# Attention of a fused kernel in a fixed order on every engine, with fixed PSUM banks and keys scaled in place

## The chip, the cores and the metric

The kernel runs on one core of a Trainium2 chip. The metric is the time of one execution on the device in microseconds (us); lower is better. The engines are PE (TensorE), DVE (VectorE), ACT (ScalarE), POOL (GpSimd) and SP (SyncE, which issues most DMAs). L12 means line 12 of the kernel, of before or of the change as the sentence says.

## The reference

A causal linear attention with a decay for each head comes first. Its output, laid out as 4 × 768 rows of 512, goes through a Fourier mix, a normalisation and an MLP.

```python
# attention: q, k, v are (4, 8, 768, 64), lam (8,); blocks of 64 rows
for b in range(nb):
    intra = einsum(qb, kb) * Dmask[None]                # Dmask = lam ** (i - j) for i >= j
    intra = einsum(intra, vb)
    inter = einsum(qb * lam_pow[None], kv_state)
    out[:, :, sl] = intra + inter
    kv_state = lam_block * kv_state + einsum(kb * rev_pow[None], vb)
# mix: x is (4, 768, 512), w_ch1 (512, 2048), w_ch2 (2048, 512)
mixed = np.real(fft(fft(x, axis=1), axis=2))
u = x + mixed
un = (u - mean(u)) / sqrt(var(u) + 1e-6)
return u + np.maximum(un @ w_ch1, 0.0) @ w_ch2
```

The two weights arrive as float64 and are converted to float32 on the chip.

## The kernel before

**Attention** runs in twelve steps: step i is batch i // 3, rows 256 (i % 3) to 256 (i % 3) + 255, as two chunks of 128 rows. For one step PE does:

- `turn_k`, `turn_q` (L349, L356): 16 transposes of keys and queries; ACT copies them out (L350, L357), and DVE makes the decayed queries (L361, L363);
- `to_state` (L369): products of the scaled keys `kd` with v, which DVE adds to the state (L380; L377 for the first chunk of a batch). POOL scales the old state by the decay of a chunk ahead of that (L379). There are three state buffers in turn;
- `from_state` (L399): decayed queries with the state of before, which opens the output's PSUM tile `po`;
- `scores` (L384): keys with queries in four PSUM tiles, which DVE masks with the decay (L390) into `sc`;
- `within` (L405): masked scores with v, added into `po`; ACT copies the result out (L411 and the lines behind it);
- `back` (L425): transposes of the output of the step before; ACT writes the halves into x (L435, L436).

POOL prepares a step in `apart`: it copies keys and queries into layouts split by even and odd rows (L341, 1024 elements wide; ACT does it for step 0) and writes the scaled keys into the one buffer `kd` (L343). SP loads k, q and v, 512 KB each (L330), up to three steps ahead, into three rotating buffers `ld` and two for v.

**What is woven in.** Between these pieces the program emits other work: the Fourier mix of batch 0 (`fft_ln`: folds on DVE L549 to L637; matmuls along the sequence L670; along the width L682 to L687; sums L758 to L771; statistics and normalisation L701 to L722; transposes L727); the conversion of the weights, 32 *words* of 512 KB (five DVE instructions L230, L234, L236, L238, L239 and two of ACT, L229 and L232, for each); and the first half of the MLP (`mlp`: L816 first product, L830 second, L860 and L861 the sums). `mixed` and `beside` interleave the generators by weights, of which each `yield` states how much work it stands for.

**What sets the order.** The program order is that of emission, and a scheduler may move instructions unless `tc.keep_in_program_order` pins them. Before, only the first product of each group on PE and some instructions of DVE are pinned. `tc.high_priority` favours the instructions behind which PE waits.

**PSUM.** There are eight banks, in two pools: `pa` with five and `pm` with three tiles in rotation. Attention, Fourier mix and MLP take them in turn; `psum_t` chooses the pool by a count.

**Behind attention** the rest of the first half of the MLP runs beside the Fourier mix of batches 1 to 3 and the remaining words, and then the second half and the other products. PE stays in one stream to the end (L1265, L1191 and L1098 are matmuls there).

Of the kernel before, what the change touches and what calls it, by code (L numbers as in the profile page):

```python
# [19 lines left out]
EPS = 1e-6  # L20
# [57 lines left out]
def kernel(  # L78
# [44 lines left out]
    ld = front_pool("ld", 3)  # L123
# [14 lines left out]
    cnt = [0]  # L138

# [3 lines left out]

    def psum_a(shape):
        return new(pa, shape, "pa")

    def psum_m(shape):
        return new(pm, shape, "pm")
# [5 lines left out]
    nc.scalar.dma_start(lamb, lam.rearrange("(o h) -> o h", o=1).broadcast_to([128, H]))  # L154
# [5 lines left out]
    nc.gpsimd.memset(pulse, 0.0)  # L160
    for hd in HD:
        nc.vector.tensor_copy(pulse[hd, 1:C + 1:2], ident[hd, hd])
    decay = const.tile([128, H, C + 1], F32, name="decay")
    for h in range(H):
        scan(decay[:, h, :], lamb[:, h:h + 1].broadcast_to([128, C + 1]), pulse, 0.0, op0=ALU.mult, op1=ALU.add)

    lamq = const.tile([128, HP], F32, name="lamq")
    for hi in range(2):
        nc.vector.tensor_copy(lamq[HD[hi]], lamb[HD[hi], hi::2])
    qpow = const.tile([128, HP, C], F32, name="qpow")  # L170
    for hp in range(HP):
        scan(qpow[:, hp, :], lamq[:, hp:hp + 1].broadcast_to([128, C]), ident, 1.0, op0=ALU.mult, op1=ALU.bypass)
# [3 lines left out]
    nc.gpsimd.memset(cvt, -896.0 * 16 * 8)  # L176
    mhalf = const.tile([128, G], F32, name="mhalf")
    nc.gpsimd.memset(mhalf, -0.5)
# [19 lines left out]
    def load_tables(i):  # L198
        if i == 1:
            nc.sync.dma_start(cs, cn["cs"].ap())  # L200
            nc.sync.dma_start(ix, cn["ix"].ap())
        elif i == 2:
            nc.sync.dma_start(dt, cn["dt"].ap())

    def load_weights(dst, src):

        if src.dtype == F32:
            nc.sync.dma_start(dst, src)
            yield 1.0
            return  # L210
        if landed[0] < NW // 2:
            raw = hp_.tile([128, 2 * WP], U32, tag="hr", name=f"raw{cnt[0]}")
        else:
            raw = ld.tile([128, 2 * WP], U32, tag="kqv", name=f"raw{cnt[0]}")
        e = ep.tile([128, 2 * WP], U16, tag="e", name=f"e{cnt[0]}")
        pw, sg = e[:, 0:WP], e[:, WP:2 * WP].bitcast(BF16)
        cnt[0] += 1
        nc.sync.dma_start(raw, src.bitcast(U32))
        if LAG[0] <= landed[0] < LAG[1] or NW // 2 <= landed[0] < NW // 2 + 2:
            yield 0.5  # L220
# [3 lines left out]


        held_back = LAG[0] <= landed[0] < LAG[1] or NW // 2 <= landed[0] < NW // 2 + 2
        landed[0] += 1
        pin = tc.keep_in_program_order if late_words else lambda i: i
# [1292 lines left out]
```

## Time and profile before

| what | value |
|---|---|
| runs | 818.54, 813.4, 814.37 us; median 814.37 us |
| profiled execution | 816.04 us, its span 814.3 us, mean PE clock 0.972 of full speed |
| busy, share of the span | PE 756.0 us (93%), DVE 612.6 us (75%), ACT 225.6 us (28%), POOL 195.9 us (24%) |
| instructions | 17075 |
| DMA | 123.50 MB, mean 152 GB/s |

The profile shows one execution. A busy time is a union of intervals, and a matmul of the program leaves two records on PE. Line numbers in it are those of the kernel before. An idle time is put down to what ended last before the waiting instruction started. The granted clock of PE is given for any stretch of time as a share of full speed.

### The profile page before, as it was taken

What the parts mean: (1) busy time and instruction counts of PE and PEld (TensorE: products, weight loads), DVE (VectorE), ACT (ScalarE), POOL (GpSimd) and SP (SyncE); (2) the same over time, 40 slices, a digit from 0 to 9 for tenths busy, and PEclk for the clock granted to TensorE, in tenths of its full rate; (3) what the DMA queues carried; (4) which work ended last, traced back from release to release, by engine and by line L of the source; (5) the groups of instructions that cost most, each with busy time, mean ns of one, the idle gap of its engine ahead of it and who ended that gap; (6) DMA issues with size and microseconds to landing.
All of it is one profiled execution on the core that took longest, in us unless ns stands there. A gap on an engine that the chain in (4) does not pass through costs nothing.

```text
span 814.3 us, 17075 instructions
## 1 busy us (share of the span) xinstructions
PE 756.0 (93%) x6872; PEld 657.1 (81%) x6872; DVE 612.6 (75%) x1173; ACT 225.6 (28%) x512; POOL 195.9 (24%) x215
## 2 busy tenths in 40 slices
PE   4796777969999998999999999999999999999997
PEld 3785767757658676865974789999999999999997
DVE  4568678973199767846695699978997599758984
ACT  3462434552236211100200122103420343123410
POOL 4433241420000120421100693244012200330013
PEclk9798998988999998999999999999999999999999
DMA  9764645461345244742143236667554556455442
GB/s 260 237 177 126 181 138 183 144 221 59 126 140 178 75 97 110 226 98 97 57 88 89 79 142 214 221 222 230 176 182 129 178 174 182 134 175 172 131 144 77
DMA packets 119220, 123.50 MB, mean 152 GB/s; under 512 B 40174, under 2 KB 79726, under 8 KB 119142
## 3 DMA queue, kind: packets, MB, share of 16 engines
q1 hardware_dynamic: 111792, 103.13, 43.3%
q0 software_dynamic: 4032, 12.99, 4.7%
q10 hardware_dynamic: 3318, 6.30, 2.2%
q8 instruction: 54, 0.88, 0.4%
q14 instruction: 24, 0.20, 0.1%
HBM read 90.66 MB, written 31.73 MB: 150 GB/s over the span
## 4 chain that ended last, share of the span: by engine, by line
PE 73%; DVE 14%; DMA 6%; POOL 3%; issue 2%; ACT 1%; SPq 0%; DVEq 0%; ACTq 0%; POOLq 0%
PE p L1265 20%; PE p L1191 16%; PE pm L830 10%; PE pm L816 9%; PE p L1098 5%; PE pa L670 4%; DMA raw<-in_moe_w_ch_dram 2%; PE pa L384 1%; PE pa L405 1%; DVE un L722 1%; DVE e L230 1%; DMA w<-in_v_dram 1%; DVE w L236 1%; DMA x<-xb,ix 1%; DVE stt L701 1%
## 5 line engine op out<-in xcount | busy, mean ns | idle before, releaser
L816 PE MATMUL pm<-ut,w 128*128 128x256 f32 x512 | 117.0, 384 | 0.5 <-DVE hr L822 0.5
L816 PEld LDWEIGHTS pm<-ut,w 128*128 128x128 f32 x512 | 96.9, 192 | 16.7 <-issue 3.5
L830 PE MATMUL pm<-w,hr 128*128 128x512 f32 x240 | 106.4, 595 | 1.7 <-DVE hr L822 1.7
L830 PEld LDWEIGHTS pm<-w,hr 128*128 128x128 f32 x240 | 45.1, 191 | 53.0 <-issue 50.1
L1286 POOL TENSOR_TENSOR y<-y,u 128x512 f32<-128x512 f32 x12 | 19.9, 1661 | 187.1 <-DVE y L1295 155.5
L1265 PE MATMUL p<-tx,sx 128*128 128x128 f32 x400 | 52.7, 275 | 0.0
L1265 PEld LDWEIGHTS p<-tx,sx 128*128 128x128 f32 x400 | 48.7, 192 | 0.0
L1200 DVE TENSOR_TENSOR ha<-p,ha 128x512 f32<-128x512 f32 x60 | 40.1, 685 | 8.3 <-PE p L1191 8.1
L1271 ACT COPY y<-p 128x128 f32<-128x128 f32 x48 | 12.8, 266 | 103.6 <-PE p L1265 103.1
L824 ACT ACTIVATE hr<-pm 128x256 f32<-128x256 f32 x44 | 16.7, 378 | 84.1 <-PE pm L816 82.9
L384 PE MATMUL pa<-w 64*64 64x128 f32 x608 | 28.8, 284 | 11.1 <-DVE w L390 4.5
L1273 DVE TENSOR_TENSOR y<-p,y 128x128 f32<-128x128 f32 x92 | 25.5, 285 | 16.3 <-PE p L1265 9.3
L1265 PE MATMUL p<-w,ha 128*128 128x128 f32 x288 | 37.4, 275 | 0.0
L1200 DVE TENSOR_TENSOR hs<-p,hs 128x512 f32<-128x512 f32 x39 | 26.2, 685 | 12.3 <-PE p L1191 12.3
L1265 PEld LDWEIGHTS p<-w,ha 128*128 128x128 f32 x288 | 34.9, 192 | 0.1
L384 PEld LDWEIGHTS pa<-w 64*64 64x64 f32 x608 | 24.6, 139 | 12.6 <-DVE w L390 5.0
L1191 PE MATMUL p<-sx,tx 128*128 128x128 f32 x264 | 33.9, 275 | 0.0
L232 ACT ACTIVATE e<-e,cvt 128x512 uint16<-128x512 uint16 x32 | 22.9, 721 | 34.3 <-DVE e L230 34.3
L1191 PEld LDWEIGHTS p<-sx,tx 128*128 128x128 f32 x264 | 31.6, 192 | 0.0
L343 POOL TENSOR_TENSOR w<-kqv,decay 128x1024 f32<-128x1024 f32 x12 | 23.6, 1968 | 32.2 <-PE pa L369 22.5
L805 POOL DMA_INDIRECT out_dram<-y,ix x12 | 13.7, 1145 | 67.9 <-DVE y L865 56.4
L229 ACT ACTIVATE e<-raw 128x512 bf16<-128x512 int16 x32 | 21.7, 679 | 28.4 <-DMA raw<-in_moe_w_ch_dram 11.8
(326 smaller groups left out, 1943.4 us busy)
## 6 DMA issues: line engine op xcount, KB each, us to landing
tx<-td SPq DMA_DIRECT2D x84, 256.0 KB
raw<-in_moe_w_ch_dram SPq DMA_DIRECT2D x32, 512.0 KB
tx<-sd SPq DMA_DIRECT2D x63, 256.0 KB
kqv<-in_k_dram SPq DMA_DIRECT2D x12, 512.0 KB
kqv<-in_q_dram SPq DMA_DIRECT2D x12, 512.0 KB
w<-in_v_dram SPq DMA_DIRECT2D x12, 512.0 KB
td<-tx SPq DMA_DIRECT2D x21, 256.0 KB
ud<-x SPq DMA_DIRECT2D x16, 256.0 KB
```

The source lines that it names most:

```text
L229: pin(nc.scalar.activation(sg, top.bitcast(I16), AF.Sign))
L232: nc.scalar.activation(pw, pw, AF.Relu, bias=cvt[:, 0:1], scale=8.0)
L343: nc.gpsimd.tensor_tensor(kd, kt, w, op=ALU.mult)
L384: lead(mm(pss[hi][r][HD[ch], hp, :], lhsT=kT[HD[hi], r, hp, D * ch:D * ch + D], rhs=qT[HD[hi], hp, C * ch:C * ch + C], start=True, stop=Tr ...
L670: mm = nc.tensor.matmul(ps[:, n, :], lhsT=piece(a, i, n), rhs=cs[0:rows, a, i in (2, 3), n, :], start=(a == 0), stop=(a == 1))
L816: nc.tensor.matmul(ps, lhsT=w1[:, c, 128 * fc:128 * fc + 128], rhs=ut[:, c, :], start=(c == 0), stop=(c == KO - 1))
L830: return nc.tensor.matmul(ps, lhsT=hr[(fc - f0) // 4][:, fc % 4, 128 * i:128 * i + 128], rhs=w2[:, fc, :], start=(fc == f0), stop=(fc == f ...
L1098: nc.tensor.matmul(ps, lhsT=s2.A[a][:, kt, 128 * i:128 * i + 128], rhs=U[b][:, kt, :], start=(first and kt == 0), stop=(kt == 1), skip_gro ...
L1191: nc.tensor.matmul(ps[:, 128 * i:128 * i + 128], lhsT=ab[m][0][:, 128 * i:128 * i + 128], rhs=ab[m][1], start=(start and i == 0), stop=Tru ...
L1200: V.tensor_tensor(o, p, o, op=ADD)
L1265: nc.tensor.matmul(ps[:, 0:HM // 2], lhsT=ab[m][0][i], rhs=ab[m][1][:, i, :], start=(start and i == 0), stop=(i == HF // 2 - 1), skip_grou ...
L1273: V.tensor_tensor(o, ps[:, 0:HM // 2], o, op=ADD)
```

## The change

The change fixes, up to the end of attention, what stands where on each engine, and rearranges a few steps.

- **Order.** A helper `P` pins every instruction while `strict[0]` is true, which it is until `run(att)` has ended.
- **PSUM.** The eight banks are tiles with roles: four rotate for transposes, products to the state, scores and `back`; two hold `po`; two rotate for Fourier mix and MLP. Behind attention the pools rotate as before.
- **Buffers.** The rotating pool `ld` becomes three fixed buffers: two hold keys of even and odd steps, one the queries. Keys are scaled in place (L373 of the change) instead of into `kd`; the split copies `k2` and `q2` (L372) have one buffer each.
- **Start.** `load_first` loads the first k and q straight into the split layout, in runs of 256 bytes; no copy on ACT is needed for them.
- **State.** The decay of the state (`decayed`, L418) is emitted one chunk ahead: behind the add of the first chunk in `to_state`, and behind `from_state` for the second.
- **Old-state products last.** `scores` (L423) comes ahead of `from_state` (L438), except in the last step.
- **Words.** Raw words are fetched one ahead, and more of them are converted early: six up to the masking of step 4, twelve up to that of step 11. In each, DVE's first instruction comes ahead of ACT's. Of the MLP, two L816 groups, two L830 products and one transposing group fewer stand in attention.
- **Smaller.** Weights of `mixed` and places of `yield` change, `norm(1)` of batch 0 comes ahead of the second `wide`, and tables load a step later.

The core of the diff:

```diff
-    ld = front_pool("ld", 3)
+    ld = front_pool("ld", 1)
...
+    def P(i):
+        return keep(i) if strict[0] else i
...
+    banks = [new(pa, [128, 512], "pa") for _ in range(5)] + [new(pm, [128, 512], "pm") for _ in range(3)]
+    turn = {"s": 0, "m": 0, "o": 0}
...
+    def psum_t(shape):
+        turn["s"] += 1
+        return held_bank((turn["s"] - 1) % 4, shape)
+
+    def psum_o(shape):
+        turn["o"] += 1
+        return held_bank(4 + (turn["o"] - 1) % 2, shape)
+
     def psum_a(shape):
+        if strict[0]:
+            turn["m"] += 1
+            return held_bank(6 + turn["m"] % 2, shape)
         return new(pa, shape, "pa")
...
-    kd = flat(w2[:, FS + 6:FS + 8, :])
+    k_of = [t.rearrange("p (h r d) -> p h r d", h=H, r=2) for t in words[0:2]]
+    q_of = words[2].rearrange("p (h r d) -> p h r d", h=H, r=2)
+    k2, q2 = (w2[:, FS + i:FS + i + 2, :].rearrange("p (r c) m -> p r (c m)", r=2) for i in (4, 6))
...
+        kd = k_of[i % 2]
+        if i:
+            for t, src in ((k2, kd), (q2, q_of)):
+                P(nc.gpsimd.tensor_copy(t.rearrange("p r (h d) -> p r h d", h=H), src.rearrange("p h r d -> p r h d")))
+        P(nc.gpsimd.tensor_tensor(kd, kd if i else by_head(k2), w, op=ALU.mult))
...
-                    nc.gpsimd.tensor_tensor(s_new, s_old, spow.broadcast_to([128, HP, D]), op=ALU.mult)
-                    nc.vector.tensor_tensor(s_new, s_new, pu[ch], op=ALU.add)
+                    P(nc.vector.tensor_tensor(s_new, s_new, pu[ch], op=ALU.add))
+                if c < NC - 2 and ch == 0:
+                    decayed(c + 1)
...
         def begin(i):
-            from_state(i)
-            yield 1.2
-            scores(i)
-            yield 2.2
...
+            first_ = from_state if i == n - 1 else scores
+            first_(i)
+            (scores if i == n - 1 else from_state)(i)
+            if i % SC < SC - 1:
+                decayed(2 * (i % SC) + 2)
...
-    run(mixed((until(att, lambda: (0, 0) in xs), 40.0), (w, 3.0)))
+    run(mixed((until(att, lambda: (0, 0) in xs), 33.0), (w, 6.0)))
...
-    run(mixed((lead_half, t_half - 37.0), (fr, 62.0), (w, 0.5 * NW)))
+    strict[0] = False
+    run(until(w, lambda: landed[0] == NW // 2))
+    run(mixed((lead_half, t_half - 13.0), (fr, 62.0), (w, 0.5 * NW)))
```

**DVE around the masking of the scores.** The first rows are DVE's of before in step 4: the folds of the first Fourier mix (L549 to L633; `fe` and `fo` are their even and odd halves) and the masking (L390).

```order
L549 TENSOR_TENSOR fe_687<-x_502,x_906 128x512
L550 TENSOR_TENSOR fo_688<-x_502,x_906 128x512
L552 TENSOR_TENSOR fe_687<-fe_687 128x255
L553 TENSOR_TENSOR fo_688<-fo_688 128x255
L623 TENSOR_TENSOR fe_687<-fe_687 128x257
L624 TENSOR_TENSOR fe_687<-fe_687 128x257
L390 TENSOR_TENSOR w_134<-pa_1010,decay 128x512
L390 TENSOR_TENSOR sc_137<-pm_1012,decay 128x512
L628 TENSOR_TENSOR fe_687<-fe_687 128x2x128
L629 TENSOR_TENSOR fe_687<-fe_687 128x2x128
L390 TENSOR_TENSOR w_134<-pa_1011,decay 128x512
L390 TENSOR_TENSOR sc_137<-pa_1013,decay 128x512
```

The next rows are DVE's of the change in step 4: two adds to the state (L413), the first two folds (L586, L587), the masking (L429), and behind it a word (L257 to L264).

```order
L413 TENSOR_TENSOR st_136<-st_136,pa_97 128x256
L413 TENSOR_TENSOR st_137<-st_137,pa_98 128x256
L586 TENSOR_TENSOR fe_661<-fo_662,x_654 128x512
L587 TENSOR_TENSOR fo_662<-fo_662,x_654 128x512
L429 TENSOR_TENSOR w_142<-pa_99,decay 128x512
L429 TENSOR_TENSOR sc_148<-pa_96,decay 128x512
L429 TENSOR_TENSOR w_142<-pa_97,decay 128x512
L429 TENSOR_TENSOR sc_148<-pa_98,decay 128x512
L257 TENSOR_SCALAR e_1006<-raw_812 128x512
L260 TENSOR_SCALAR w_142<-raw_812 128x512
L261 SCALAR_TENSOR_TENSOR w_142<-raw_812,w_142 128x512
```

Fourteen folds stood ahead of the masking of step 4; two stand there now, and the other folds follow in later steps. In steps 1, 2, 3 and 8 of the change one whole word stands between L413 and L429:

```order
L413 TENSOR_TENSOR st_138<-st_138,pa_98 128x256
L257 TENSOR_SCALAR e_560<-raw_477 128x512
L260 TENSOR_SCALAR w_142<-raw_477 128x512
L261 SCALAR_TENSOR_TENSOR w_142<-raw_477,w_142 128x512
L263 TENSOR_TENSOR e_560<-e_560 128x512
L264 SCALAR_TENSOR_TENSOR w_142<-w_142,e_560 128x512
L429 TENSOR_TENSOR w_142<-pa_99,decay 128x512
```

These rows are from step 2. Before, a word stood there in step 1 and the last three instructions of one in step 2.

**POOL in the first steps.** The rows of before, from the copies for step 2 on (`kqv` keys and queries, `w_135` the scaled keys or the split queries, `st` the states):

```order
L341 COPY kqv_458<-kqv_292 128x1024
L341 COPY w_135<-kqv_294 128x1024
L343 TENSOR_TENSOR w_135<-kqv_292,decay 128x1024
L379 TENSOR_TENSOR st_129<-st_128,qpow 128x256
L379 TENSOR_TENSOR st_130<-st_129,qpow 128x256
```

The same stretch in the change (`words_144` and `words_145` are keys, `words_146` queries, `w_143` their split copies):

```order
L418 TENSOR_TENSOR st_137<-st_136,qpow 128x256
L418 TENSOR_TENSOR st_138<-st_137,qpow 128x256
L372 COPY w_143<-words_144 128x1024
L372 COPY w_143<-words_146 128x1024
L373 TENSOR_TENSOR words_144<-words_144,decay 128x1024
```

The two decays of the state moved from behind the scaling of the keys to ahead of the copies, and the scaling now writes into the buffer that it reads.

More of the change, by code (lines that the diff above doesn't have):

```diff
@@ L138, with keep @@
     cnt = [0]
+    strict, pinned = [True], {}
+    def keep(i):
+        if id(i) not in pinned:
+            pinned[id(i)] = i
+            tc.keep_in_program_order(i)
+        return i
+    def P(i):
+        return keep(i) if strict[0] else i
     def new(pool, shape, tag, **kw):
@@ new lines, in weights @@
+        raws = {}
+        for j, (dst, src) in enumerate(todo):
+            if src.dtype == F32:
+                P(nc.sync.dma_start(dst, src))
+                landed[0] += 1
+                yield 1.0
+                continue
+            for a in (j, j + 1):
+                if a not in raws and (a == j or a < NW // 2):
+                    raws[a] = fetch(a, todo[a][1])
+            held_back = NW // 2 <= j < NW // 2 + 2
+            if held_back or j == 0:
+                yield 0.5
+            convert(j, raws[j], dst)
+            landed[0] += 1
+            yield 0.5 if held_back or j == 0 else 1.0
@@ L258, with block_sums @@
     sums_of = {}
-    def block_sums(eng, queue, k, t, stage, inside, pin=tc.keep_in_program_order):
+    def block_sums(eng, queue, k, t, stage, inside, pin=keep):
         Q11, Q12, Q21, Q22 = quarters_w(t)
@@ L304 @@
     sc = (sc0, sc1)
-    bank_of = [0]
-    def psum_t(shape):
-        bank_of[0] += 1
-        if early[0] and bank_of[0] % 8 in (1, 4, 6):
-            return psum_m(shape)
-        return psum_a(shape)
-    early = [True]
-    kqv, po = {}, {}
+    po = {}
     mm = nc.tensor.matmul
@@ L345, in turn_k @@
     def turn_k(i):
-        k2 = kqv.pop((i, "k2"))
         for r in range(2):
             pt = psum_t([128, HP, 128])
-            lead(nc.tensor.transpose(pt[:, hp, :], k2[:, r, 128 * hp:128 * hp + 128], ident) for hp in range(HP))
-            nc.scalar.copy(kT[:, r], pt)
+            lead(P(nc.tensor.transpose(pt[:, hp, :], k2[:, r, 128 * hp:128 * hp + 128], ident)) for hp in range(HP))
+            P(nc.scalar.copy(kT[:, r], pt))
     def turn_q(i):
-        q2 = kqv.pop((i, "q2"))
         for r in range(2):
@@ L355, in turn_q @@
             pt = psum_t([128, HP, 128])
-            lead(nc.tensor.transpose(pt[:, hp, :], q2[:, r, 128 * hp:128 * hp + 128], ident) for hp in range(HP))
-            nc.scalar.copy(qT[:, :, r::2], pt)
+            lead(P(nc.tensor.transpose(pt[:, hp, :], q2[:, r, 128 * hp:128 * hp + 128], ident)) for hp in range(HP))
+            P(nc.scalar.copy(qT[:, :, r::2], pt))
             with tc.high_priority(100):
@@ L779, in fft_ln @@
         for t, after in ((1, 2), (2, 0)):
+            if t == 1 and b in LEADS:
+                yield from norm(1)
             now = wide(after)
-            if t == 1:
+            if t == 1 and b not in LEADS:
                 yield from norm(1)
@@ L848, in mlp @@
                 ps = split[i]
-                tc.keep_in_program_order(second(ps, i, f1 - 1))
+                keep(second(ps, i, f1 - 1))
             else:
@@ L918, in keep_sums @@
     def keep_sums(k):
-        pin = tc.keep_in_program_order
+        pin = keep
         B11, B12, B21, B22 = quarters_b(s2.B[PRODUCTS[k][1]])
@@ L962, in load_u @@
             if j == 0:
-                tc.keep_in_program_order(i)
+                keep(i)
     def bank():
```

368 lines of the change are left out of this document (180 added, 188 removed).

## The prediction

> **What bounds the kernel now.** I first split the span at 206.2 us, where the last product of attention ends. The columns behind the length are busy times of PE, PEld, DVE, ACT and POOL with instruction counts, then PE's granted clock, the DMA share and GB/s.
>
> ```profile
> 0.00:206.20 206.20, 158.91 (x2963) 139.86 (x2963) 141.44 (x261) 90.44 (x197) 67.63 (x74) 0.91 0.57 173
> 206.20:814.30 608.10, 597.09 (x3910) 517.28 (x3910) 471.19 (x912) 135.18 (x315) 128.26 (x141) 0.99 0.48 144
> ```
>
> Behind attention PE is busy 597.09 of 608.10 us: there only less PE work would help, and the change takes none away. Inside attention PE is idle for 206.20 − 158.91 = 47.3 us, and its mean clock is 0.91. So what can be won lies in the first quarter. Next I read PE's timeline there for its long idle times; in brackets stands the idle time ahead of the row and what ended it.
>
> ```profile
> 7.38 0.87 PE L349 MATMUL pm<-ident,kqv 128*128 128x128 f32 x3 [7.38 <-ACT kqv L341]
> 18.83 0.66 PE L349 MATMUL pm<-ident,kqv 128*128 128x128 f32 x4 [2.25 <-DVE st L380]
> 23.39 0.90 PE L356 MATMUL pa<-ident,w 128*128 128x128 f32 x3 [3.37 <-DVE sc L390]
> 37.74 1.26 PE L369 MATMUL pa<-w 64*64 64x64 f32 x30 [2.35 <-DMA w<-in_v_dram]
> 73.19 1.09 PE L356 MATMUL pa<-ident,w 128*128 128x128 f32 x4 [5.21 <-DVE w L390]
> 80.82 0.33 PE L399 MATMUL pm<-w,st 64*64 64x128 f32 x2 [1.21 <-DVE st L380]
> 89.16 0.63 PE L356 MATMUL pa<-ident,w 128*128 128x128 f32 x4 [4.47 <-DVE w L390]
> 123.36 0.64 PE L356 MATMUL pm<-ident,w 128*128 128x128 f32 x4 [3.84 <-DVE w L390]
> 141.31 1.98 PE L384 MATMUL pa<-w 64*64 64x128 f32 x30 [2.24 <-DVE mv L702]
> 176.80 1.76 PE L384 MATMUL pa<-w 64*64 64x128 f32 x44 [2.05 <-ACT oT L411]
> 183.07 1.39 PE L384 MATMUL pa<-w 64*64 64x128 f32 x11 [4.51 <-DVE w L390]
> ```
>
> These eleven make 38.9 of the 47.3 us. Five of them end with DVE's masking of the scores (L390): 3.37 + 5.21 + 4.47 + 3.84 + 4.51 = 21.4 us, the largest item. DVE itself was not waiting then. Its timeline shows two such places:
>
> ```profile
> 18.35 0.42 DVE L380 TENSOR_TENSOR st<-st,pm 128x256 f32<-128x256 f32 x1 [5.66 <-POOL st L379]
> 18.69 0.89 DVE L230 TENSOR_SCALAR e<-raw 128x512 uint16<-128x512 uint16 x1
> ...
> 21.44 0.69 DVE L239 SCALAR_TENSOR_TENSOR w<-w,e 128x512 f32<-128x512 f32 x1
> 22.05 0.68 DVE L390 TENSOR_TENSOR w<-pm,decay 128x512 f32<-128x512 f32 x1
> ...
> 64.67 0.69 DVE L549 TENSOR_TENSOR fe<-fo,x 128x512 f32<-128x512 f32 x1
> ...
> 72.03 0.42 DVE L624 TENSOR_TENSOR fe<-fe 128x257 f32<-128x257 f32 x1
> 72.36 0.68 DVE L390 TENSOR_TENSOR w<-pa,decay 128x512 f32<-128x512 f32 x1
> ```
>
> At 18.69 one whole word (L230 to L239, five instructions, 22.05 − 18.69 = 3.36 us) stands ahead of L390, and PE waits 3.37 us. At 64.67 it is a row of folds, 72.36 − 64.67 = 7.7 us, and PE waits 5.21 us. The windows show what such waits cost besides:
>
> ```profile
> 39.00:42.60 3.60, 3.60 (x77) 3.60 (x71) 3.35 (x4) 0.00 (x0) 1.92 (x1) 0.59 0.11 29
> 69.90:76.70 6.80, 3.50 (x22) 3.13 (x24) 6.80 (x14) 3.01 (x8) 1.04 (x1) 0.55 0.01 2
> 141.60:145.00 3.40, 3.40 (x42) 3.07 (x37) 3.40 (x9) 1.35 (x3) 1.41 (x3) 0.60 0.00 0
> 179.00:189.30 10.30, 6.23 (x33) 5.08 (x34) 5.12 (x10) 2.93 (x6) 0.00 (x0) 0.53 0.17 48
> ```
>
> In these four stretches the clock is at about half, and each lies on or right behind one of the waits. They hold 24.1 us, of which PE is busy 16.7, or 0.69. Over the whole stage (1 − 0.91) × 206.2 = 18.6 us of clock are missing; the busy share of it is about 13 us. Idle time and clock together make some **60 us that better feeding could win at the very most**.
>
> [...]
>
> **The change, part by part**, against the profiled execution (816.04 us, span 814.3; the median of the runs is 1.7 us lower).
>
> *(a) DVE's order.* Every instruction is pinned up to the end of attention, and folds and words are cut into pieces. In the order of the changed kernel the rows between the state's adds (L413) and the masking (L429) are: in steps 1, 2, 3 and 8 one word; in 5, 6 and 7 six to eight folds; in steps 0 and 9 nothing; in 4 two folds; in 10 and 11 more (e). A word was 3.36 us above; eight folds at 0.4 to 0.7 us are as much. So seven steps keep a piece like that at 18.69, which cost 3.37 us of PE. PE's next transposes take the banks of these scores, so they wait for L429 as they did for L390. In the change's favour, PE now has the scores before the products of the old state, and 'within' of the step before beside the piece. Ends: nothing (all hidden) and 7 × 3.37 = 23.6 us. I take half, 1.7 us a step, **12 us in place of 21.4: −9.4** (−21.4 to +2.2).
>
> *(b) Keys and states on POOL.*
>
> ```profile
> POOL w L343 <- PE pa L369: 22.5, 8, 4.9
> DVE st L380 <- POOL st L379: 14.6, 5, 5.7
> L341 POOL COPY kqv<-kqv 128x1024 f32<-128x1024 f32 x11 | 11.8, 1075 | 37.4 <-issue 16.6 <-PE pa L349 8.4 <-DMA kqv<-in_k_dram 7.3
> L379 POOL TENSOR_TENSOR st<-st,qpow 128x256 f32<-128x256 f32 x16 | 11.3, 706 | 10.9 <-DVE st L380 6.4 <-DVE st L377 2.8 <-PE pa L399 1.7
> ```
>
> The one buffer of scaled keys makes POOL wait for PE (22.5 us), the decay of the state (L379) is queued behind it, and DVE waits 14.6 us for that; 2.25 + 1.21 = 3.5 us of it reach PE. In place in two buffers, with the decay issued early, these go. New: the decay behind the second step of a batch waits for the last old-state product that reads its buffer, and the copy of the next keys (L372) is queued behind it, and the transposes wait for that. That is 0.71 + 1.08 = 1.8 us, once in each of four batches, 7.2 us at most and nothing if woven FFT or MLP products cover it. Such products stand there in the last batches, so I take three of the four, +5.4. Net **+1.9** (−3.5 to +3.7).
>
> *(c) Loads.* The second buffer of q, k and the words are fixed, so SP no longer holds v behind k and q that wait for POOL: the wait of 2.35 us at 37.74 goes, **−2.35** (0 to −2.35).
>
> *(d) The start.*
>
> ```profile
> 6.19 1.04 ACT L341 COPY kqv<-kqv 128x1024 f32<-128x1024 f32 x1 [3.71 <-DMA kqv<-in_k_dram]
> 7.99 1.05 ACT L341 COPY w<-kqv 128x1024 f32<-128x1024 f32 x1 [0.75 <-DMA kqv<-in_q_dram]
> ```
>
> The first k and q come already split, so two ACT copies of 1.04 us go. k lands at 6.19 and q 1.8 us later. At the same rate PE gains 1.1 us, less what POOL's first scaling then sets; at half the rate q lands 2 × 1.8 us later than now and the loss is 2.5 us. The run length is half of that before, and I take **−0.2** (−1.1 to +2.5). [...]
>
> *(e) Steps 10 and 11.* In step 10 a word, four statistics and seven sums stand between L413 and L429:
>
> ```profile
> L701 DVE BATCH_NORM_STATS2 stt<-x 128x6 f32<-128x512 f32 x6 | 4.0, 677 | 0.0
> ```
>
> 3.36 + 4 × 0.68 + 7 × 0.42 (the L860 row of (g) has a sum of this kind) come to some 9 us, with two matmul groups of the width transform and 'within' beside them. The two banks for FFT and MLP have fixed roles, so the next MLP group waits for those sums. Ends 0 and 8 us; I take **+4**. Of the waits of before, those of 2.24 and 2.05 us stay.
>
> *(f) Clock.* Eleven waits cost 13 us, or 1.2 to 1.5 us each. I count five left that are over 2.2 us, 7 us: **−6** (0 to −13).
>
> *(g) What moves behind attention.* By the order, two groups of L816, two products of L830 and one transposing group fewer stand in attention, and four words are still to be converted at its end.
>
> ```profile
> L816 PE MATMUL pm<-ut,w 128*128 128x256 f32 x512 | 117.0, 384 | 0.5 <-DVE hr L822 0.5
> L830 PE MATMUL pm<-w,hr 128*128 128x512 f32 x240 | 106.4, 595 | 1.7 <-DVE hr L822 1.7
> 219.77 0.42 DVE L860 TENSOR_TENSOR x<-pm,x 128x256 f32<-128x256 f32 x1 [16.59 <-PE pm L830]
> ```
>
> 117.0 / 64 groups = 1.83 us and 106.4 / 128 products = 0.83 us, so with the transposes some 5.9 us of PE work change their place: attention ends 18 us earlier where the span gains 12. DVE has 16.59 us idle ahead of 219.77, and four words are 13.4 us: covered, **0**. If the cover fails, its price is up to 13.4 us.
>
> Sum: −9.4 + 1.9 − 2.35 − 0.2 + 4 − 6 + 0 = **−12.1**, so 804.0 in the profiled execution's count, and 814.37 − 12.1 = **802** on the median of the runs.
>
> **The rivals.**
> - *PE fed nearly throughout.* The pieces are hidden beside 'within' and scores: (a) −18, (e) 0, (f) −10, the rest as above: −28.7, some **786**. For it: PE's work beside a piece is about as long as the piece. Against: in 0 to 206.2 us DVE is busy 141.44 us already, so a late piece is not soon made up.
> - *The stalls change their names.* Words stand where folds stood: (a) +2.2, (f) −3, the rest as above, or (g) fails by 10 us: −12.1 + 10. Both end within a few us of 814: say **812 to 817**. For it: the piece at 18.69 cost all of its 3.36 us, and the ACT half of a word (L258, L259) now stands in order behind the copies of 'within' (L453 to L460), with the word's last instructions and L429 waiting for it.
> - That the order isn't carried out is no rival: the rows in the section on the change show it.
> - *Pinned words hold the queue.* Before, the scheduler could let L390 pass a word whose raw data were late; with every instruction pinned, a late transfer stops DVE, with L429 and L395 behind it, and then PE.
>
> ```profile
> DVE e L230 <- DMA raw<-in_moe_w_ch_dram: 4.1, 2, 3.4
> ```
>
> DVE waited for raw words only twice, 4.1 us in all. In the changed order twelve words lie in attention, six of them ahead of the masking of step 4. At 2.05 us (4.1 / 2) for each of twelve, 24.6 us come on top: −12.1 + 24.6 = +12.5, some **827**. It decides from 12.1 / 12 = 1.0 us a word for a loss at all, and from 1.7 us (20.2 us in all) for one over 1%. Against it: raw words are fetched one ahead, a whole word of time early.
>
> **How the numbers follow.** Within 1% means 806.2 to 822.5, about what a measurement of this kernel can tell from no change. Forecast (790 to 811): 0.47, of which 0.41 lie below 806.2. Fed throughout: 0.14. Stalls renamed: 0.23. Queue held: 0.16, nearly all of it above 822.5. So faster 0.55, same 0.29, slower 0.16. The range is 784 to 823: below lies half of the optimistic case, 0.07, above most of the last one, 0.13.
>
> **What the changed profile would show.** (a) and (f): PE's idle time up to the last L444 falls from 47 to about 33 us, L429 ends waits of 1 to 2 us, and the mean clock there rises to 0.94 or more. (b) no wait of L413 on L418 over 1 us, and a wait of L384 on L372 of about 2 us once in a batch. (c) no wait of L403 on a DMA. (e) one wait of about 4 us of PE near step 10. (g) attention ends near 188 us, and PE is still full behind it. I am wrong if L429 still ends waits of 3 to 5 us (then renamed), if L257 or L258 waits for raw words in most steps (then held), or if PE shows gaps behind 188 us that before did not have.

## The result and the profile after

The changed kernel took 803.62 us (median of 6 runs, 799.66 to 806.95) against 814.32 us before; the ratio is 0.9868, with a 95% interval of 0.9831 to 0.9904. Its profiled execution took 804.96 us, with a span of 803.2 us and a mean clock of 0.983. The forecast was 802 us.

The stage up to the last product of 'within' (L444 now) and the rest, in the columns of the first fence of the prediction, are in the changed kernel:

```profile
0.00:188.88 188.88, 146.01 (x2913) 130.48 (x2913) 136.88 (x240) 80.44 (x180) 67.24 (x74) 0.93 0.62 181
188.88:803.20 614.32, 605.63 (x3960) 522.77 (x3960) 480.49 (x934) 143.53 (x331) 128.19 (x141) 1.00 0.49 145
```

Attention ends 17.3 us earlier (206.2 to 188.9) and the rest is 6.2 us longer (608.1 to 614.3), so 11.1 us of span are left. PE's idle time in attention fell only from 47.3 to 188.88 − 146.01 = 42.9 us. Its busy time fell by 12.9 us, and that is work that moved behind attention, not a better clock. PE's rows for the MLP up to the end of attention are these, the first two before, the last one in the change:

```profile
L816 PE MATMUL pm<-ut,w 128*128 128x256 f32 x64 | 17.2, 417 | 0.0
L830 PE MATMUL pm<-w,hr 128*128 128x512 f32 x11 | 5.4, 611 | 0.0
L855 PE MATMUL pm<-ut,w 128*128 128x256 f32 x32 | 11.0, 507 | 4.1 <-DVE ds L796 4.1
```

L855 is L816 of before. A group leaves eight records, so PE ran eight groups there before and four now, not two fewer as the section on the change has it; of the second product it ran about five matmuls before (ten or eleven records) and none now. By the prediction's rows (117.0 us for 512 records, 106.4 us for 240) that is 7.3 + 4.4 us. With the transposing group, some 12 us moved, by this estimate, and not 5.9.

PE's clock was at 0.50 in seven stretches of attention before (the first from 21.44 us, the last to 188.70) and in eight of the change (41.53 to 181.48). The sums over these stretches, before and in the change:

```profile
sum 37.54, PE 26.71 PEld 24.29 DVE 28.45 ACT 11.94 POOL 9.63; mean PE 3.82 PEld 3.47 DVE 4.06 ACT 1.71 POOL 1.38
sum 27.28, PE 27.28 PEld 24.61 DVE 15.79 ACT 9.10 POOL 3.49; mean PE 3.41 PEld 3.08 DVE 1.97 ACT 1.14 POOL 0.44
```

The time at half clock fell by 10.3 us. But before, PE was idle for 10.8 us of it, and in the change it is busy throughout. By the granted 0.50 the clock costs half of the busy part: 13.4 us before and 13.6 us now. Eight transposes (L384) take 1.94 us at 55.19 us, in such a stretch, and 1.09 us at 68.67 us, outside one. Behind attention before has one more such stretch, and the change has none in which PE works:

```profile
314.99:321.82 6.83, 6.83 (x22) 6.48 (x21) 4.77 (x12) 1.52 (x3) 0.60 (x1) 0.50 0.46 156
```

So the 11.1 us are made up as follows. In attention PE idles 4.4 us less, and the clock costs 0.3 us more. Behind it PE idles 2.3 us less (8.7 us in place of 11.0), and the clock costs 3.4 us less. The other 1.3 us are the difference between the work that left attention (12.9 + 0.3 = 13.2 us) and the work that came behind it (8.5 us more busy time + 3.4 = 11.9 us), both counted at full clock. Each side of this account is one execution; whether other executions of before have the stretch at 315 us is not known.

PE's waits up to 215 us (line and operand that waited, engine and line waited for; us in total, times, longest):

```profile
PE pa L384 <- DVE w L429: 11.0, 4, 4.7
PE pa L384 <- POOL w L372: 6.7, 4, 1.8
PE pm L764 <- DVE un L759: 5.2, 2, 3.1
PE pa L384 <- DMA w<-in_k_dram: 5.1, 1, 5.1
PE pa L403 <- issue: 5.1, 4, 2.3
PE pm L855 <- DVE ds L796: 4.1, 1, 4.1
PE pa L423 <- DVE st L413: 1.9, 3, 1.0
PE pa L403 <- DMA w<-in_v_dram: 0.9, 1, 0.9
```

The masking (L429, once L390) still ends the largest wait. Its four waits are 0.7, 1.70, 3.86 and 4.70 us; the two long ones are

```profile
55.19 1.09 PE L384 MATMUL pa<-ident,w 128*128 128x128 f32 x4 [3.86 <-DVE w L429]
96.11 1.27 PE L384 MATMUL pa<-ident,w 128*128 128x128 f32 x5 [4.70 <-DVE w L429]
```

Ahead of the first, a word takes from 48.32 to 54.37 us, 6.05 us, of which DVE waits 0.54 us for ACT; ahead of the second, eight folds take from 89.72 to 95.28 us. POOL's copies and scaling (L372, L373) run beside both, from 49.17 to 53.89 and from 89.01 to 93.29 us. Two folds of 128x257 and 128x256 take 1.26 and 2.02 us there (L661, L665); the five behind POOL's work, 128x255 and 128x256, take 0.41 to 0.42 us each. Next in the list come the transposes' waits for the split keys (L372), which before did not have. Behind "issue" is no lack of instructions. DVE, POOL and PE around 70 us of the changed kernel, from their timelines, show what it is:

```profile
67.91 0.99 DVE L257 TENSOR_SCALAR e<-raw 128x512 uint16<-128x512 uint16 x1
68.81 1.26 DVE L260 TENSOR_SCALAR w<-raw 128x512 uint32<-128x512 uint32 x1
70.11 2.29 DVE L261 SCALAR_TENSOR_TENSOR w<-raw,w 128x512 f32<-128x512 uint32 x1
...
73.38 1.28 DVE L395 TENSOR_TENSOR w<-pa,qpow 128x512 f32<-128x512 f32 x2
```

```profile
67.58 2.22 POOL L372 COPY w<-words 128x1024 f32<-128x1024 f32 x2
69.76 2.09 POOL L373 TENSOR_TENSOR words<-words,decay 128x1024 f32<-128x1024 f32 x1
```

```profile
74.17 1.09 PE L403 MATMUL pa<-w,words 64*64 64x64 f32 x30 [2.35 <-issue]
```

A word stands between L429 and L395, and it runs from 67.91 to 73.38, 5.5 us in place of the 3.36 us at 18.69 before. Even those were longer than with POOL idle: L230 and L234 took 0.89 and 0.84 us there, beside POOL's L341 and L379 (18.27 to 20.07 us), and the same two instructions of the change (L257, L260) take 0.41 us each at 56.76 us, where POOL is idle. The whole word takes 2.5 us there; these are the first and the last instruction of the word before this one in the change:

```profile
56.76 0.41 DVE L257 TENSOR_SCALAR e<-raw 128x512 uint16<-128x512 uint16 x1
58.60 0.69 DVE L264 SCALAR_TENSOR_TENSOR w<-w,e 128x512 f32<-128x512 f32 x1
```

L260 and L261 lie beside POOL's instructions: L261 takes 2.29 us against 0.69 us at 57.54 us, where POOL is idle. L395 reads a bank of the four that rotate. The first of its two ends at 74.06 us, and L403 starts at 74.17 us after 2.35 us of idle time. That L403 waits for this bank is inferred from these times and from the rotation; the profile doesn't name it.

### The profile page after: what moved, and what is told of

It is laid out like the page before. It is cut to its first block, busy times and chain, and to the rows that moved or that the text cites. A ratio compares the mean times of both kernels' runs of the same rounds, so it can differ in the third digit from the quotient of the medians.

```text
span 803.2 us, 17083 instructions
## 1 busy us (share of the span) xinstructions
PE 751.6 (94%) x6872; PEld 653.3 (81%) x6872; DVE 617.4 (77%) x1173; ACT 224.0 (28%) x510; POOL 195.4 (24%) x215
## 4 chain that ended last, share of the span: by engine, by line
PE 79%; DVE 8%; issue 3%; POOL 3%; ACT 2%; DMA 2%; SPq 0%; ACTq 0%; DVEq 0%; POOLq 0%
PE p L1304 21%; PE p L1230 16%; PE pm L869 12%; PE pm L855 12%; PE p L1137 5%; PE pa L707 2%; PE pa L403 2%; POOL w L372 1%; PE pa L384 1%; DMA words<-in_moe_w_ch_dram 1%; PE pm L707 1%; PE pa L390 1%; PE pa L464 1%; PE pa L423 1%; DVE w L264 1%
## 5 line engine op out<-in xcount | busy, mean ns | idle before, releaser
L855 PE MATMUL pm<-ut,w 128*128 128x256 f32 x512 | 119.9, 388 | 6.4 <-DVE ds L796 4.1
L855 PEld LDWEIGHTS pm<-ut,w 128*128 128x128 f32 x512 | 97.5, 194 | 24.8 <-issue 8.6
L384 PE MATMUL pa<-ident,w 128*128 128x128 f32 x96 | 16.0, 316 | 22.9 <-DVE w L429 11.0
L384 PEld LDWEIGHTS pa<-ident,w 128*128 128x128 f32 x96 | 12.3, 160 | 25.7 <-issue 17.3
L844 POOL DMA_INDIRECT out_dram<-y,ix x12 | 13.6, 1133 | 79.1 <-DVE y L904 67.0
L423 PE MATMUL pa<-w 64*64 64x128 f32 x768 | 27.3, 282 | 2.8 <-DVE st L413 1.9
L423 PEld LDWEIGHTS pa<-w 64*64 64x64 f32 x768 | 24.0, 140 | 5.2 <-DVE st L413 3.0
```

The lines of the kernel that those rows point to most:

```text
L384: lead(P(nc.tensor.transpose(pt[:, hp, :], k2[:, r, 128 * hp:128 * hp + 128], ident)) for hp in range(HP))
L423: lead(P(mm(pss[r][hi][HD[ch], hp, :], lhsT=kT[HD[hi], r, hp, D * ch:D * ch + D], rhs=qT[HD[hi], hp, C * ch:C * ch + C], start=True, stop= ...
L855: P(nc.tensor.matmul(ps, lhsT=w1[:, c, 128 * fc:128 * fc + 128], rhs=ut[:, c, :], start=(c == 0), stop=(c == KO - 1)))
```

## The experiments

The ratios are to the kernel before. The first four runs were made together on one chip, then the next four, the next three, and the last; the change itself stands at 0.9868 (0.9831 to 0.9904).

| run | edit of the changed kernel | median us | ratio, 95% interval |
|---|---|---|---|
| old_first | from_state ahead of scores | 807.39 | 0.9914 (0.9890 to 0.9937) |
| unpinned | DVE, ACT, POOL not pinned | 803.94 | 0.9867 (0.9819 to 0.9916) |
| decay_late | decay right ahead of the add | 804.25 | 0.9875 (0.9840 to 0.9909) |
| rotating | old_first with rotating banks | 813.52 | 0.9993 (0.9968 to 1.0017) |
| one_op_words | 12 words in one instruction each | 785.2 (one run) | |
| copy_first | L372 ahead of the second decay | 799.82 | 0.9818 (0.9772 to 0.9864) |
| word_behind_queries | no woven work ahead of L384 | 804.10 | 0.9884 (0.9838 to 0.9931) |
| start_as_before | first k, q as before | 801.50 | 0.9856 (0.9799 to 0.9914) |
| words_as_before | word weights as before | 804.92 | 0.9883 (0.9853 to 0.9913) |
| copy_first_old_start | both | 800.20 | 0.9837 (0.9784 to 0.9890) |
| copy_first_act | copy_first, queries split on ACT | 798.75 | 0.9816 (0.9779 to 0.9852) |
| all_words_inside | 16 words in attention, not 12 | 817.96 | 1.0041 (1.0018 to 1.0065) |

My theory was the account of the prediction: shorter pieces ahead of the masking, held in place by the pins, and a better clock. The rivals were that the gain comes from the buffers and banks, or from the order of PE alone.

### The order of the two products

```diff
-            first_ = from_state if i == n - 1 else scores
-            first_(i)
-            (scores if i == n - 1 else from_state)(i)
+            from_state(i)
+            scores(i)
```

> The changed kernel with from_state ahead of scores in every step, as before; all else as in the change. My account: the masking L429 starts 0.9 us later (the length of from_state) while the next transposes come right behind the scores, so PE waits for L429 some 1 us longer in most of 12 steps, and the decay of the state, which is issued behind from_state, comes earlier, so the four waits on L372 (6.7 us in the profile of the change) shrink to under 2 us. Net +3 to +8 us against the change (803.6), so 807 to 812. Rival (the order of the two products is of no account, only pins and banks are): within 2 us of 803.6, with the waits on L372 unchanged.

807.39 us: 3.8 us more than the change, inside the account's range, though the two intervals still overlap a little. The last L444 ends at 192.9 us, 4.1 us later than in the change. Where the waits are is different from what I expected: L429 ends only 8.0 us of them, and the waits on L372 are gone, but `from_state` now waits for ACT's copies of the output (L450 to L458) in several steps:

```profile
PE pa L384 <- DVE w L429: 8.0, 3, 3.6
...
PE pa L438 <- ACT oTs L455: 2.4, 2, 1.3
PE pm L438 <- ACT oT L450: 2.2, 2, 1.2
PE pa L438 <- ACT oT L450: 1.9, 3, 0.7
```

With scores in between, as in the change, no wait of L438 for ACT shows. But these waits only take the place of others, as the stage as a whole shows:

```profile
0.00:192.94 192.94, 151.70 (x2913) 131.95 (x2913) 134.74 (x241) 80.41 (x180) 66.60 (x74) 0.89 0.61 177
```

PE is idle for 192.94 − 151.70 = 41.2 us here and for 42.9 us in the change. What grew, by 5.7 us, is the time of the same 2913 records, at a mean clock of 0.89 in place of 0.93. So the stage is longer by its clock. Which of the waits brings that about was not isolated.

### The pins

```diff
-        return keep(i) if strict[0] else i
+        return keep(i) if strict[0] and i.ins.engine not in (nc.vector.engine, nc.scalar.engine, nc.gpsimd.engine) else i
```

> The changed kernel with PE and SP pinned, but DVE, ACT and POOL left to the scheduler again (but for the instructions that were pinned before); banks, buffers and steps as in the change. My account: folds and words stand ahead of L429, L395 or L413 again where the scheduler took them, waits of PE on L429 and L395 grow from 11 us to 17 us or more, and the time is 808 to 814. Rival (the gain comes from the buffers, the banks and the order of PE): within 2 us of 803.6.

803.94 us, the same as the change: the rival was right. The stage ends at 188.5 us. The waits change their names, and little of their sum; the view is that of PE's waits again:

```profile
PE pa L423 <- DVE st L413: 10.4, 6, 4.7
PE pa L384 <- DVE w L429: 7.0, 4, 4.2
...
PE pm L438 <- ACT oT L450: 4.2, 1, 4.2
```

In some steps the scheduler puts words ahead of L413, where the fixed order has them ahead of L429. It also puts more of them into attention. A word ends with L264, and up to 183 us, ahead of the last maskings, DVE has done 14 words here, against 12 in the change ahead of its last maskings:

```profile
L264 DVE SCALAR_TENSOR_TENSOR w<-w,e 128x512 f32<-128x512 f32 x14 | 10.4, 740 | 0.2
```

With two more words inside, the stage is as short. Pinning DVE, ACT and POOL by itself brings nothing here; the pins on PE stayed.

### The early decay

```diff
                 else:
+                    decayed(c)
                     P(nc.vector.tensor_tensor(s_new, s_new, pu[ch], op=ALU.add))
-                if c < NC - 2 and ch == 0:
-                    decayed(c + 1)
...
-            if i % SC < SC - 1:
-                decayed(2 * (i % SC) + 2)
```

> The changed kernel with the decay of the state on POOL issued right ahead of each add, behind the scaling of the keys (L373), as before. My account: L413 waits 8 to 15 us in all for L418, of which 3 to 5 us reach PE, and the 6.7 us of waits of the transposes on L372 go; net -3 to +3 us against 803.6. Rival (the early decay carries the gain): +6 us or more, with waits of L423 or L438 on L413 in most steps.

804.25 us: no difference, as the account said. The two waits trade places (L428 is the masking here):

```profile
PE pa L384 <- DVE w L428: 18.6, 7, 4.0
```

The 6.7 us on L372 are gone, and the masking's waits rose by 7.6 us.

### The banks

The edit replaces the fixed banks by the two rotating pools and the count of before, with from_state first:

```diff
     def psum_t(shape):
         turn["s"] += 1
-        return held_bank((turn["s"] - 1) % 4, shape)
+        if early[0] and turn["s"] % 8 in (1, 4, 6):
+            return new(pm, shape, "pm")
+        return new(pa, shape, "pa")
...
     def psum_o(shape):
-        turn["o"] += 1
-        return held_bank(4 + (turn["o"] - 1) % 2, shape)
+        return psum_t(shape)
...
-        return psum_a(shape) if strict[0] else new(pm, shape, "pm")
+        return new(pm, shape, "pm")
```

> Everything pinned as in the change, but the PSUM tiles rotate over two pools of five and three banks as before, and from_state comes ahead of scores (fixed order of products as in old_first, with which this is to be compared). My account: the roles of the banks are of little worth: the wait of L855 (4.1 us) on the sums shrinks, others come; within 4 us of old_first. Rival (the roles carry the gain): 6 us or more slower than old_first, with new waits of PE on PSUM tiles that DVE or ACT still read.

813.52 us, 6.1 us slower than old_first; the two intervals are apart. So the banks matter, as the rival had it, but not where it looked for it. The last L444 ends at 192.2 us here and at 192.9 us in old_first. The loss comes behind it. First rotating, then old_first, from there to 220 us:

```profile
192.20:220.00 27.80, 23.56 (x87) 16.24 (x84) 16.81 (x39) 13.63 (x28) 2.36 (x2) 0.88 0.50 163
```

```profile
192.90:220.00 27.10, 27.10 (x107) 17.53 (x104) 19.69 (x46) 15.19 (x31) 2.17 (x2) 1.00 0.57 186
```

PE is idle for 4.2 us and the clock is at 0.88. In PE's timelines of rotating and of old_first the reason is an order:

```profile
192.16 1.99 PE L854 MATMUL pm<-ut,w 128*128 128x256 f32 x8
198.39 1.09 PE L763 MATMUL pa<-ident,un 128*128 128x128 f32 x4 [4.24 <-DVE un L758]
```

```profile
192.87 1.99 PE L854 MATMUL pm<-ut,w 128*128 128x256 f32 x8
194.86 3.70 PE L868 MATMUL pm<-w,hr 128*128 128x512 f32 x8
198.40 0.60 PE L763 MATMUL pm<-ident,un 128*128 128x128 f32 x4
```

In old_first, 3.70 us of the MLP's second product stand ahead of the transposes that wait for DVE; in rotating they come behind. With 4.2 us idle and 0.12 × 27.8 = 3.3 us of clock, most of the difference is named (9.0 us between the two profiled executions, 6.1 us between the medians). Why the second product could not be placed there (no free tile of the pool, I suppose) was not measured.

### What words cost in attention

```diff
+        if j < 12:
+            P(nc.vector.tensor_scalar(d, hi, 0x000FFFFF, 0x00100000, op0=ALU.bitwise_and, op1=ALU.bitwise_or))
+            return
```

> The changed kernel, in which the first twelve words are not converted: of the five DVE and two ACT instructions of each, one DVE instruction (L260) is left, so the MLP has other weights. Only the stage up to the last L444 is read (188.9 us in the change, L429 ends 11.0 us of PE's waits there, and 5.1 us more of L403 stand behind L395). If DVE's pieces ahead of the masking and of L395 set PE's waits: 16 us of waits and 4 to 8 us of half clock go, and the last L444 ends at 165 to 172 us. Rival (POOL's copies, the states and PE's own work set the pace of a step, and DVE is off the path): not before 182 us.

The last L444 (L447 here) ends at 168.67 us, inside the account's 165 to 172:

```profile
0.00:168.67 168.67, 137.99 (x2913) 124.38 (x2913) 101.19 (x193) 65.77 (x156) 66.35 (x74) 0.97 0.70 204
```

Twelve words, with their ACT instructions, cost the stage 188.9 − 168.7 = 20.2 us, about 1.7 us each, where one takes 2.5 us on DVE when POOL is idle. PE's idle time is 30.7 us in place of 42.9, so 12.2 of the 20.2 us are waits and the rest is nearly all clock (0.97 in place of 0.93). The 1.7 us is the figure that the prediction took for a step, but there it stood for waits alone. Of the 16 us of waits in the account only part went: the masking still ends 6.3 us, and L403's waits on "issue" fell from 5.1 to 0.9 us.

### POOL's copies first

```diff
-            if i % SC < SC - 1:
-                decayed(2 * (i % SC) + 2)
...
+            if i % SC:
+                decayed(2 * (i % SC))
         P(nc.gpsimd.tensor_tensor(kd, kd if i else by_head(k2), w, op=ALU.mult))
```

> The changed kernel with the second decay of the state issued on POOL behind the two split copies (L372) and ahead of the scaling (L373), not ahead of the copies. The four waits of the transposes on L372 (6.7 us) should go. If they add to the rest: 4 to 8 us faster than the change, so 796 to 800. Rival (PE then waits for L429 in the same places, as in decay_late, where L429's waits rose from 11.0 to 18.6 us when those on L372 went): within 2 us of 803.6.

799.82 us, 3.8 us less, just short of the account's 4 to 8; the interval overlaps that of the change, so the runs alone don't settle it. The stage ends at 186.2 us, 2.7 us earlier. The copies run before the decay's wait:

```profile
23.18 2.22 POOL L372 COPY w<-words 128x1024 f32<-128x1024 f32 x2
26.46 0.76 POOL L420 TENSOR_TENSOR st<-st,qpow 128x256 f32<-128x256 f32 x1 [1.06 <-PE pa L440]
```

and the 6.7 us are gone from PE's waits, of which part comes back:

```profile
PE pa L386 <- DVE w L431: 13.3, 7, 4.0
...
PE pa L425 <- DVE st L415: 4.1, 4, 1.5
```

That is 2.3 and 2.2 us more (L431 the masking, L415 the add). L466, the `back` transposes, also waits 4.0 us for ACT's copies (L387), and the waits of L405 (L403 in the change) on "issue" fell from 5.1 to 0.9 us.

### The word ahead of the queries

```diff
-            yield 1.0
             if i + 1 < n:
                 turn_k(i + 1)
...
-            yield 2.0
+            yield 3.0
```

> The changed kernel with the place for woven work ahead of the transposes (between L429 and L395) merged into the one behind them (between L395 and L413). A word there stretched to 5.4 us beside L373 at 67.9 and 161.2 us and held L395, so that L403 waited 2.35 us twice. If that is so: the 5.1 us of waits of L403 go, with some half clock: 3 to 7 us faster, 797 to 801. Rival (the word then holds L413 and with it L423 and L438 as long): within 2 us of 803.6, with waits on L413 in place of those of L403.

804.10 us, no gain; the rival was right. L403's waits fell from 5.1 to 2.1 us, and those of the scores on the add rose from 1.9 to 7.6 us:

```profile
PE pa L423 <- DVE st L413: 7.6, 4, 3.2
...
PE pa L403 <- issue: 2.1, 6, 0.8
```

### The start

```diff
     def load_first():
...
-            for r in range(2):
-                P(nc.sync.dma_start(t[:, r].rearrange("p (h d) -> p h d", h=H), s_[:, r]))
+        load(0, "kq")
+        for t, src in ((k2, k_of[0]), (q2, q_of)):
+            P(nc.scalar.copy(t.rearrange("p r (h d) -> p r h d", h=H), src.rearrange("p h r d -> p r h d")))
```

> The changed kernel with the start of before: k and q of step 0 loaded in runs of 512 bytes into the buffers of keys and queries, and split by two ACT copies. In the change the first transposes start at 5.14 us, before at 7.38. My account: +0.2 to +2 us, since the first L403 waits for POOL's scaling and for v either way (10.49 us now, 10.98 before). Rival (the start sets all that follows): +2.2 us and more, the whole of the first transposes' delay.

801.50 us; the intervals overlap widely, so no effect of the start shows, and the rival fell. ACT's first copy in start_as_before begins at 6.12 us, when the whole of k is there. In the change PE starts at 5.14 us on the first half, but the first L403 starts at 10.49 us against 10.92 us here. The 2.2 us won at the transposes are 0.4 us at L403.

### Where words stand, and how many

```diff
-    run(mixed((until(att, lambda: (0, 0) in xs), 33.0), (w, 6.0)))
+    run(mixed((until(att, lambda: (0, 0) in xs), 40.0), (w, 3.0)))
...
-    run(mixed((mix, 24.0), (att, 2.2 * t_step), (w, 1.1)))
+    run(mixed((mix, 24.0), (att, 2.2 * t_step), (w, 4.0)))
```

> The changed kernel with the weights by which words are woven in as before (3.0 in place of 6.0, then 1.0 and 4.0): three words up to the masking of step 4 in place of six, and two words ahead of the masking in steps 7, 8 and 10 of the order. The total in attention is nearly the same (eleven in place of twelve). My account: steps 1 and 2 lose a piece each and gain 2 to 4 us, the later steps with two words wait 3 to 5 us each; +2 to +8 us against 803.6. Rival (only the total of DVE's work counts, not its place): within 2 us.

804.92 us, 1.3 us more than the change, with overlapping intervals: nothing that this measurement can tell. The masking's waits rose from 11.0 to 16.5 us, and the wait of L855 fell from 4.1 to 0.8 us.

In the last run only one weight is raised, and all sixteen words stand inside:

```diff
-    run(mixed((mix, 24.0), (att, 2.2 * t_step), (w, 1.1)))
+    run(mixed((mix, 24.0), (att, 2.2 * t_step), (w, 8.0)))
```

> The changed kernel with all sixteen words of the first half of the weights ahead of the last masking, as before, in place of twelve (the weight of the words beside the end of the first Fourier mix is 8.0 in place of 1.1); PE's work in attention is the same. Account after the runs so far: twelve words cost attention 20.2 us (188.9 against 168.7 in one_op_words), 1.7 us each, and the words behind attention cost nothing since PE is full there. So four more inside should make attention 5 to 8 us longer, and the whole 808 to 812. Rival (words are free as long as they don't stand ahead of a masking, or what they take is given back behind attention, where DVE then has 13 us less to do): within 2 us of 803.6.

817.96 us, 14.4 us more than the change and more than before. The direction was as expected; the size was about twice that. The stage is 13.3 us longer, of which 8.8 us are idle time of PE:

```profile
0.00:202.17 202.17, 150.52 (x2913) 133.09 (x2913) 147.82 (x257) 85.27 (x188) 67.75 (x74) 0.89 0.60 176
```

Three words stand ahead of one masking, from 141.01 to 151.97 us; the masking behind them and PE's wait:

```profile
151.97 0.68 DVE L429 TENSOR_TENSOR w<-pa,decay 128x512 f32<-128x512 f32 x1
```

```profile
152.80 1.94 PE L384 MATMUL pa<-ident,w 128*128 128x128 f32 x8 [7.97 <-DVE w L429]
```

That one wait is 8.0 us. So the run has two changes at once, four words more and three of them in one step, and it doesn't tell their shares. Hardly anything of it came back behind attention, though DVE had four words less to do there: 815.5 − 202.2 = 613.3 us against 614.3 in the change.

### Versions that go further

copy_first with the edit of start_as_before:

> copy_first with the start of before (two ACT copies). The start was of no account by itself (ratio to before 0.9856 against 0.9868): so 798 to 802, as copy_first (799.8). Rival (the 256-byte runs take the bandwidth from v and the first words, and copy_first lets that show): 795 to 797.

800.20 us: as copy_first, so again no effect of the start shows.

copy_first with the queries' split copy on ACT:

```diff
-                P(nc.gpsimd.tensor_copy(t.rearrange("p r (h d) -> p r h d", h=H), src.rearrange("p h r d -> p r h d")))
+                copy = nc.gpsimd.tensor_copy if t is k2 else nc.scalar.copy
+                P(copy(t.rearrange("p r (h d) -> p r h d", h=H), src.rearrange("p h r d -> p r h d")))
```

> copy_first with the split copy of the queries on ACT, not POOL. If POOL's work stretches the words on DVE (one took 5.4 us beside L372 and L373, 3.4 us elsewhere) and so sets L429's waits (13.3 us in copy_first): these fall to about 8 us, and the time is 795 to 798. Rival (the copy on ACT stands ahead of L385, so the transposes' copies and L395 come later by its 1.04 us): L464 and L403 wait for ACT, 801 to 806.

798.75 us, the lowest of all, though its interval overlaps that of copy_first. In its profiled execution (792.9 us of span, the shortest of its runs, 794.71 to 801.47 us) attention ends at 179.0 us and L429 (L432 here) ends 9.3 us of waits:

```profile
PE pa L387 <- DVE w L432: 9.3, 5, 3.5
```

The waits of the masking fell from 13.3 us, nearly as the theory of POOL's share said; the gain in time over copy_first is 1.1 us, which these runs don't separate from nothing. Against the kernel before, both versions are faster, by 1.8% (1.4 to 2.3% for copy_first).

## Why the prediction was right, and where it was not

The forecast was −12.1 us for the profiled execution, and −11.1 us were measured. The time and the direction held. The parts did not: several terms were off in both directions, so that the number came out so near is in part luck.

- **(a) DVE's order.** The size held, the picture behind it did not. 12 us of waits behind the masking were forecast, as 1.7 us in each of seven steps. L429 ends 11.0 us, in four waits of which the longest are 3.86 and 4.70 us, and 5.1 us of L403 behind L395 come on top, which I had not seen. The two long waits stand behind pieces that took longer beside POOL's work (a word 6.05 us in place of 2.5, two folds 1.26 and 2.02 us in place of 0.4), and the sum had no term for that; the 3.36 us that it took for a word held some of it unseen. I also ascribed the improvement to the pinned order and the cut pieces, and unpinned shows that the scheduler does as well without pins on DVE, ACT and POOL.
- **The words.** Four words fewer stand inside attention than before, and I did not write down what that saves; it was hidden in (a). A word inside costs 1.7 us on average (one_op_words), and four more, three of them in one step, cost 13.3 us (all_words_inside). But their number alone doesn't set the time, since unpinned has two more words inside than the change and as short a stage. So how much of the gain the four words bring is not shown.
- **(g) Moved work.** The forecast called the four words behind attention covered and gave them 0 us, which held: PE is idle for 8.7 of 614.3 us behind 188.9 us. The size of the moved PE work was wrong: some 12 us, not 5.9. The part behind attention grew by only 6.2 us because it also lost 2.3 us of idle time and 3.4 us of half clock, for which the sum had nothing. The count of two groups and two products was too low, and 106.4 / 128 divides the time of 240 records by the number of products that leave 256.
- **The order of scores and from_state** stood in (a) as one sentence in the change's favour. By the medians it is worth 3.8 us (4.1 us at the end of the stage), and not by shorter waits as I thought: without it PE's idle time doesn't grow, but its clock falls.
- **(b) POOL.** +5.4 us were forecast for the transposes' waits, and they are 6.7 us in four waits of at most 1.8 us, at the place that was named and once in each batch. Removing them gained 3.8 us by the medians (copy_first), with overlapping intervals. Of the other side, the waits of L413 on L418 did not all go below 1 us (6.6 us in eight, the longest 1.5), and PE waited 1.9 us for L413. The early decay, the reason for that order, is worth nothing as the change has it (decay_late); copy_first, which keeps the first early decay and has the copies ahead of the second, is 4.4 us below decay_late, again with overlapping intervals.
- **(c) Loads.** The wait of 2.35 us for v is gone; one of 0.9 us at the start is new.
- **(d) The start.** −0.2 us, measured as no difference. The half rate behind the term's loss end was the author's supposition and no run shows it; by it q would have landed at some 11.6 us (7.99 + 2 × 1.8), and the transposes of the first queries start at 7.43 us.
- **(e) Step 10.** +4 us were forecast, and L855 waits 4.10 us for L796. The waits that I said would stay (2.24 and 2.05 us) became 2.02 and 3.14 us on L764.
- **(f) Clock.** This term failed. −6 us were forecast, from five waits left and 1.2 to 1.5 us for each. In attention the clock cost 13.4 us before and 13.6 us after: eight waits are followed by a stretch at half clock, and each stretch costs 1.7 us, half of 3.41 us. What the clock gave, 3.4 us, it gave behind attention. The missing share of the whole stage (18.6 us before, (1 − 0.93) × 188.88 = 13.2 us after) did fall by 5.4 us, but it counts time in which PE is idle. The 13 us that I had worked out for the busy part before were right.
- **The signatures.** I wrote that PE's idle time would fall from 47 to about 33 us. My own terms (a) to (e) sum to −6.05 us, so it should have read 41; 42.9 us were measured. The sum itself did not use that number. The clock of the stage is 0.93 and not 0.94 or more. And one of my signs of being wrong did show: L429 still ends two waits of 3 to 5 us. In these two steps the stalls did change their names.
- **The rivals.** Pinned words that wait for raw data did not come: no wait of DVE on a raw word shows in attention, and ACT waited for one once, 5.0 us. That stalls only change their names is true of single parts (unpinned, decay_late, word_behind_queries) and of the two steps above, not of the whole.

What stays open: by the medians, undoing parts costs 14.4 us (words), 3.8 us (order) and 6.1 us (banks), more than the 10.7 us that the whole brings, so these figures can't be added up to the gain. The banks' loss lies behind attention, where before has none of it, and the words' run also bunches them. No run isolates what carries the whole. Not tried were scores first with rotating banks, the fixed banks put alone into the kernel before, and the kernel before with four words fewer in attention.

## What to carry to other kernels

When several engines take turns in a tight loop, count the foreign work that its partners carry inside the loop: here a word cost 1.7 us on average inside, and next to nothing where PE is full anyway (614.3 us behind attention in the change, 613.3 us in all_words_inside with four words fewer there), and three words in one step cost one wait of 8 us. Look also at what runs beside such work on other engines; a word took 2.5 us with POOL idle and 5.5 us beside POOL's copies and scaling. A wait that is removed at one place is won only as far as the next engine in the turn is ahead (in copy_first 6.7 us of waits went, and the stage ended 2.7 us earlier), so judge an edit by the end of the stage, not by the wait that went. Split a stage into idle time, half clock under busy time, and work that only changed its place, before an improvement of one of them is believed. And a pinned order is worth checking against the scheduler's with the same buffers: here they were equal.

## What the runs showed of the hardware

Words and folds on DVE took longer beside POOL's copies and scaling, for which the sum had no term: a word took 5.5 us beside L372 and L373 (67.91 to 73.38 us) and 2.5 us with POOL idle (56.76 to 59.29 us). In the first of these, L261 starts at 70.11 us behind L373's start at 69.76, takes 2.29 us in place of 0.69, and ends 0.55 us after L373 ends. What holds it up there is not shown.

In attention the stretches at a granted clock of 0.50 lasted 3.41, 6.83 or 10.24 us before and 3.41 us in the change. In the change each began within 1.7 us of the end of one of eight waits, of 1.70, 2.02, 2.35 (twice), 3.14, 3.86, 4.10 and 4.70 us; waits of 1.74 and 1.80 us for L372 were followed by none. So the waits of 2.02 and 2.35 us were followed by half clock here, as were those of 2.24 and 2.35 us in the prediction's rows.

Loads in runs of 256 bytes were not seen to be slower at the start than those of 512: the transposes of the first queries start at 7.43 us in the change, and in start_as_before the copy that comes ahead of them starts at 7.92 us.
